# Attention, dense layer and routed experts on one core: the hand-over from the dense layer's last chunk to expert 0 is rearranged

## The chip, the cores and the metric

The kernel runs on 1 core of one Trainium2 chip. The metric is device time in microseconds of one execution. Three runs of the kernel before took 890.3, 893.34 and 895.14 us.

## What is computed

Three layers follow one another. The first is attention with local windows and 32 global tokens. Its output, as 2176 rows of 512 numbers, goes through a dense layer with a hidden size of 2048; its activation is a leaky ReLU with a slope for each hidden unit. The third layer sends each row to one of 8 experts, 272 rows (`CAP`) to each, by a greedy choice over all gate values:

```python
# attention: out_g for 32 global tokens, out_l with |i - j| <= 32 and the global tokens
x = attention(q_l, k_l, v_l, q_g, k_g, v_g)          # -> [2176, 512]
h = x @ w_in                                         # 512 -> 2048
x = (maximum(h, 0) + alpha * minimum(h, 0)) @ w_out  # 2048 -> 512
logits = x @ w_gate                                  # 8 experts
for idx in argsort(-logits.flatten()):               # greedy, cap = 272
    tok, e = idx // 8, idx % 8
    if assigned[tok] < 0 and counts[e] < cap: assign tok to e
for e in range(8):
    out[rows of e] = maximum(x[rows of e] @ w1[e], 0) @ w2[e]   # 512 -> 1024 -> 512
```

## The kernel before

All matrix products of the dense layer and of the experts are made of three: a number is split into a rounded part and a rest (`split`, L67: a cast on ScalarE, ACT, and a subtraction on VectorE, DVE, or on GpSimd, POOL), and high times high, high times low and low times high are summed in one PSUM bank. The 2176 rows are worked on as 8 chunks of 272 (`CH`). Features lie on the partitions, rows on the free axis.

**Order of the work.** The dense layer's hidden units are taken in two halves. The first half runs beside attention. Of the second half all first products and the gate's logits are computed before any second product, so that the routing can begin early. The second products of that half are `gemm2b` (L1066): for each chunk c, four blocks of 128 output features, two at a time (d2 = 0, then 2), with the two accumulations j = 0, 1 interleaved over the hidden blocks f. At the end of each pair DVE adds the sums to the part that the first half left (`xo`). While a chunk runs, a list `post` of small jobs is worked off, one for every second f: the rows of the chunk before.

**Rows.** `rows(c, xo, q)` (L214) turns a chunk from features to rows, in blocks of 128, 128 and 16 rows (`blk`): four PE transposes into a PSUM bank (`yt`), a copy on ACT into `yr`, a DMA on the queue of SyncE (SP) to `x2d` in DRAM. The 16 left-over rows of every chunk are collected in one tile `xtail` of 128 rows, and written once, after the last chunk, by one strided DMA (L227). The bank is `px`, tag `tx`, of which there is one; only the left-over block takes another (`pH`, two banks; `p4` has two as well).

**Routing.** `router` is a generator that issues a step of a search each time that `advance(dt)` has counted enough estimated time: a group of nine small matmuls (`pc`, L795) or one (`pa`, L807) and DVE work behind each. It writes an expert's number (`EID`, L845) and its rows (`IDS`, L751).

**Experts.** `fetch_1` and `fetch_2` (L911, L922) load an expert's `w1` and `w2` in four parts each into a buffer `raw3` (pool `rw`, two buffers), and split them: cast on ACT, subtraction on POOL into the tile `m`, of 2.4 us. `fetch_x` (L903) gathers the expert's rows out of `x2d` with three indirect DMAs that POOL issues, `gather` (L932) turns each block by four transposes into a bank (`xt`, again `px`, tag `tx`) and splits it into `xsh`, `xsl`. `up` and `down` are the expert's two products, each accumulation in one of the four banks of `pH` and `p4`. Expert k+1's weights are loaded while expert k runs, as soon as the routing has named it and the weight tile is free.

**Between the two.** After the last chunk the remaining `post` jobs are worked off. `fetch_2(0)` and `fetch_x(0)` follow, then `NB0` = 20 pairs of matmuls on constants (`busy`, 512 columns each, into a bank that nobody reads) with router steps between them, then `gather(0)` with four more such matmuls behind each block. `fetch_1(1)` is then held behind the last row copy on ACT and the last gather on POOL:

```python
        for x in gather(0):
            busy(idle, ones, 4)
            advance(x + 0.9)
        with tc.issue_after(last_rows[0].ins), tc.issue_after(st.ins):
            while closed[0] < 2:
                force()
            fetch_1(1)
```

The order on PE is the order in the program (`manual_schedule`, L1054). The order on the other engines and in the DMA queues is worked out by a planner from estimated costs: an instruction whose inputs are ready can be put ahead of others that stand earlier in the program. Once planned, each engine executes in order.

Of the kernel before, what the change touches and what calls it, by code (L numbers as in the profile page):

```python
# [9 lines left out]
F32 = mybir.dt.float32  # L10
# [5 lines left out]
OP = mybir.AluOpType  # L16
# [9 lines left out]
def tile_attention_moe_moe(ctx: ExitStack, tc: tile.TileContext, qkw, vw,  # L26
                           w_in, w_out, alpha, w_gate, w1, w2, out):
    nc = tc.nc
    V, A, P, T = nc.vector, nc.scalar, nc.gpsimd, nc.tensor
    B, H, S, D, SG = BHSDG  # L30
    DM, DF = w_in.shape
    E, _, FF = w1.shape
    NTOK = B * (S + SG)
# [3 lines left out]
    KD = DM // 128  # L37
# [5 lines left out]
    KH = KF // 2  # L43
    CH = CAP
# [22 lines left out]
    def split(hi, lo, src, lo_eng=None):  # L67
        a = A.copy(hi, src)  # L68
        return a, (lo_eng or V).tensor_tensor(lo, src, hi.bitcast(F32), op=OP.subtract)  # L69
# [137 lines left out]
            yield 0.7  # L207
        X[c, hf] = None

    last_rows = [None]  # L210
    tail = {}
    blk = [(0, 128), (128, 256), (256, CH)]

    def rows(c, xo, q):  # L214
        a, b = blk[q]
        end = c == NCH - 1
        if q == 2 and not end:
            A.copy(tail["x"][:, :, 16 * c:16 * c + 16], xo[:, :, a:b])
            return
        pool, tag = (pH, "h1") if end and q == 2 else (px, "tx")  # L220
        t = pool.tile([128, DM], F32, name="yt", tag=tag)
        for k in range(KD):
            T.transpose(t[:, k * 128:(k + 1) * 128], tail["x"][:, k] if q == 2 else xo[:, k, a:b], ident)  # L223
        r = gx2.tile([128, DM], F32, name="yr", bufs=3)
        last_rows[0] = A.copy(r, t)
        if q == 2:
            nc.sync.dma_start(out=x2d.rearrange("(c r) d -> c r d", r=CH)[:, a:b], in_=r)  # L227
        else:
            nc.sync.dma_start(out=x2d[c * CH + a:c * CH + b], in_=r)

    LR = 512
    LT = KD + KH

# [342 lines left out]
    with ExitStack() as mo:  # L576
# [120 lines left out]
        gm.close()  # L697

        rt = mo.enter_context(tc.tile_pool(name="rt", bufs=2))
        rw = mo.enter_context(tc.tile_pool(name="rw3", bufs=2))  # L700
        EID = rc_.tile([128, E], I32, name="EID")
        IDS = rc_.tile([128, E, 3], I32, name="IDS")
        TT = rc_.tile([128, 2, E], F32, name="TT")
# [218 lines left out]
        def fetch_2(k):  # L922
            pool, nm = ((wa, "wa0") if k % 2 == 0 else (wb, "wb1"))
            t2 = pool.tile([128, 2, K3, DM], F32R, name="m2", tag=nm)
            w2e = w2[bass.ds(SLOT[k]["er"], 1)].rearrange("e (k p) f -> p (e k) f", p=128)
            for kk in range(0, K3, 2):
                raw = rw.tile([128, 2, DM], F32, name="raw3")
                nc.sync.dma_start(out=raw, in_=w2e[:, kk:kk + 2])
                split(t2[:, 0, kk:kk + 2], t2[:, 1, kk:kk + 2], raw, lo_eng=P)
            SLOT[k]["w2"] = t2  # L930

        def gather(k):  # L932
            d = SLOT[k]
            xh = sl.tile([128, KD, CAP], F32R, name="xsh")
            xl = sl.tile([128, KD, CAP], F32R, name="xsl")
            d["x"] = (xh, xl)
            for q, (a, b) in enumerate(SEG):
                n = b - a
                t = px.tile([128, KD, 128], F32, name="xt", tag="tx")
                for kk in range(KD):  # L940
                    T.transpose(t[:, kk, :n], d["xg"][:n, q, kk * 128:(kk + 1) * 128], ident[:n, :n])  # L941
                split(xh[:, :, a:b], xl[:, :, a:b], t[:, :, :n])
                yield 0.45 if q < 2 else 0.1

        def up(k, f):
# [91 lines left out]
        def advance(dt):  # L1037
            if wait[0] is None:
                return False
            wait[0] -= dt  # L1040
            while wait[0] is not None and wait[0] <= 0:
                x = next(route, None)
                wait[0] = None if x is None else max(wait[0], -0.3) + x * SLK
            return True
# [3 lines left out]
            advance(0)  # L1048

        HB = {}  # L1050
        NB0 = 20
        SLK, SLK2 = 1.0, 1.0
        GA = 17.5
        mo.enter_context(tc.manual_schedule(engines={mybir.EngineType.PE}))  # L1054
# [11 lines left out]
        def gemm2b(c):  # L1066
            xo = X[c, 1]
            nxt = [lambda f=f: splitg(c + 1, f) for f in range(KH)] if c + 1 < NCH else []
            if nxt:
                loadp(c + 1)  # L1070
            wo = WO[1]
            for d2 in range(0, KD, 2):
                ps = [(p4 if d2 else pH).tile([128, CH], F32, name="h2", tag="h4" if d2 else "h1") for _ in range(2)]
                for f in range(KH):
                    hi, lo = HB[c][f]
                    for j in range(2):
                        ds_ = slice((d2 + j) * 128, (d2 + j + 1) * 128)
                        for a, (w, x) in enumerate(((0, hi), (0, lo), (1, hi))):
                            T.matmul(ps[j], wo[:, w, f, ds_], x, start=f == 0 and a == 0, stop=f == KH - 1 and a == 2)  # L1079
                            if a < 2 or j == 0:  # L1080
                                yield 0.113
                    if (f % 2 == 1 if c != DEF[0] else d2 or f) and post:
                        post.pop(0)()
                        yield 0.4
                    if nxt and ((d2 == 0 and f % 2) or (d2 and f >= 2)):
                        nxt.pop(0)()
                    yield 0.113
                if "x" not in tail:
                    tail["x"] = gb_.tile([128, KD, 128], F32, name="xtail")
                for j in range(2):  # L1090
                    m = 256 if c == NCH - 1 else CH
                    V.tensor_tensor(xo[:, d2 + j, :m], ps[j][:, :m], xo[:, d2 + j, :m], op=OP.add)
                    if m < CH:
                        V.tensor_tensor(tail["x"][:, d2 + j, 16 * c:], ps[j][:, m:], xo[:, d2 + j, m:], op=OP.add)
            for q in range(3):
                post.append(lambda q=q: rows(c, xo, q))

        with tc.tile_pool(name="gb_", bufs=1) as gb_:
            NR = 14
            gr = wb.tile([128, 2, NR, CH], F32R, name="gr", tag="wb0")  # L1100
            loadp(DEF[0])
            for f in range(KH):
                splitg(DEF[0], f)
            post.pop(0)()
            for j, c in enumerate(DEF):
                for x in gemm2b(c):
                    if j or not post:
                        advance(x)
                    if closed[0] >= 1 and j >= 4 and 0 not in SLOT:
                        fetch_1(0)  # L1110
            for f in post:
                f()
                advance(0.5)
            while closed[0] < 1:
                force()
            if 0 not in SLOT:
                fetch_1(0)
        g2.close()
        sl = mo.enter_context(tc.tile_pool(name="sl", bufs=1))
        fetch_2(0)  # L1120
        while listed[0] < 1:
            force()
        st = fetch_x(0)
# [4 lines left out]
        for x in gather(0):  # L1128
            busy(idle, ones, 4)
            advance(x + 0.9)  # L1130
        with tc.issue_after(last_rows[0].ins), tc.issue_after(st.ins):
            while closed[0] < 2:
                force()
            fetch_1(1)
# [103 lines left out]
```

## Time and profile before

| | us |
|---|---|
| median of three runs | 893.34 |
| the profiled execution | 892.66 |
| its span | 890.9 |
| PE busy with matmuls | 840.3 (94%) |
| DVE busy | 531.7 (60%) |
| ACT busy | 371.6 (42%) |
| POOL busy | 350.5 (39%) |

Times in a view are microseconds from the start of the span. The profiled execution's own time is 1.8 us above its span. PE is the engine of the matmuls, PEld the loading of their weights, which goes on beside them; the ends of matmuls are modelled. PEclk is the clock granted to TensorE: 1.00 is 2.4 GHz, 0.50 is 1.2 GHz. The page shows the span in 40 slices of 22.3 us, a digit for each tenth of busy time:

```profile
PE   6989899999999899999999999999798989899995
POOL 2234320111104543400000728370767777877811
```

An arrow `<-` in brackets behind an instruction names what ended the idle time before it. "xN" is a count of like instructions merged into one row; the duration then is the whole group's.

### The profile page before, as it was taken

What the parts mean: (1) busy time and instruction counts of PE and PEld (TensorE: products, weight loads), DVE (VectorE), ACT (ScalarE), POOL (GpSimd) and SP (SyncE); (2) the same over time, 40 slices, a digit from 0 to 9 for tenths busy, and PEclk for the clock granted to TensorE, in tenths of its full rate; (3) what the DMA queues carried; (4) which work ended last, traced back from release to release, by engine and by line L of the source; (5) the groups of instructions that cost most, each with busy time, mean ns of one, the idle gap of its engine ahead of it and who ended that gap; (6) DMA issues with size and microseconds to landing.
All of it is one profiled execution on the core that took longest, in us unless ns stands there. A gap on an engine that the chain in (4) does not pass through costs nothing. (4 is left out here: it accounts for less than half of the span.)

```text
span 890.9 us, 18514 instructions
## 1 busy us (share of the span) xinstructions
PE 840.3 (94%) x7168; PEld 761.3 (85%) x7168; DVE 531.7 (60%) x1776; ACT 371.6 (42%) x872; POOL 350.5 (39%) x299
## 2 busy tenths in 40 slices
PE   6989899999999899999999999999798989899995
PEld 4768798888898899998989898997598989899995
DVE  5999955556639776565655566766566676511120
ACT  5977656455534443210100334242244444445431
POOL 2234320111104543400000728370767777877811
PEclk8999999999999999999999999999999999999999
DMA  8574514413034342201321235332455455555500
GB/s 284 192 271 155 148 43 154 120 51 117 33 116 157 108 127 94 70 8 54 98 56 45 78 112 178 91 104 81 125 147 185 144 166 179 157 165 179 180 24 36
DMA packets 50272, 107.64 MB, mean 121 GB/s; under 512 B 6729, under 2 KB 23113, under 8 KB 50185
## 3 DMA queue, kind: packets, MB, share of 16 engines
q1 hardware_dynamic: 47288, 97.56, 35.3%
q0 software_dynamic: 2896, 8.92, 2.7%
q8 instruction: 56, 0.92, 0.4%
q14 instruction: 32, 0.25, 0.1%
HBM read 88.63 MB, written 17.83 MB: 119 GB/s over the span
## 5 line engine op out<-in xcount | busy, mean ns | idle before, releaser
L69 POOL TENSOR_TENSOR m<-raw,m 128x1024 fp32r<-128x1024 f32 x64 | 152.6, 2391 | 58.8 <-ACT m L68 55.9
L168 PE MATMUL h<-xh,win 128*128 128x272 f32 x768 | 165.6, 298 | 2.2 <-DVE g L187 1.9
L168 PEld LDWEIGHTS h<-xh,win 128*128 128x128 f32 x768 | 126.4, 190 | 11.3 <-issue 6.3
L69 POOL TENSOR_TENSOR glo<-g,ghi 128x272 fp32r<-128x272 f32 x64 | 57.1, 896 | 169.2 <-ACT ghi L68 169.2
L200 PE MATMUL y<-ghi,wout 128*128 128x272 f32 x512 | 110.9, 297 | 2.7 <-ACT wout L68 1.3
L168 PE MATMUL h<-xl,win 128*128 128x272 f32 x384 | 111.8, 292 | 1.7 <-DVE xl L69 1.5
L1079 PE MATMUL h<-gr,wout 128*128 128x272 f32 x768 | 110.7, 295 | 0.0
L955 PE MATMUL h<-xsh,m 128*128 128x272 f32 x512 | 106.6, 298 | 1.9 <-ACT xsh L68 1.9
L173 DVE TENSOR_SCALAR nm<-h,al 128x272 f32<-128x272 f32 x128 | 63.5, 497 | 74.3 <-PE h L168 73.8
L69 POOL TENSOR_TENSOR gr<-gb,gr 128x272 fp32r<-128x272 f32 x64 | 48.0, 777 | 145.2 <-DVE nm L173 114.9
L68 ACT CAST m<-raw 128x1024 fp32r<-128x1024 f32 x64 | 66.9, 1049 | 88.9 <-DMA raw<-in_moe_w_dram 87.4
L971 PE MATMUL h<-hh,m 128*128 128x272 f32 x512 | 103.4, 293 | 0.0
L1079 PEld LDWEIGHTS h<-gr,wout 128*128 128x128 f32 x768 | 99.2, 188 | 0.9 <-ACT gr L68 0.4
L200 PEld LDWEIGHTS y<-ghi,wout 128*128 128x128 f32 x512 | 83.5, 189 | 8.4 <-issue 3.6
L955 PEld LDWEIGHTS h<-xsh,m 128*128 128x128 f32 x512 | 83.3, 191 | 3.2 <-ACT xsh L68 2.0
L971 PEld LDWEIGHTS h<-hh,m 128*128 128x128 f32 x512 | 81.4, 188 | 0.5 <-issue 0.2
L200 PE MATMUL y<-glo,wout 128*128 128x272 f32 x256 | 74.8, 297 | 1.4 <-POOL glo L69 1.4
L971 PE MATMUL h<-hl,m 128*128 128x272 f32 x256 | 75.5, 295 | 0.0
L168 PEld LDWEIGHTS h<-xl,win 128*128 128x128 f32 x384 | 72.9, 190 | 3.0 <-DVE xl L69 2.6
L955 PE MATMUL h<-xsl,m 128*128 128x272 f32 x256 | 75.3, 294 | 0.2 <-DVE xsl L69 0.2
L344 ACT ACTIVATE pr<-sc,mx 128x224 f32<-128x224 f32 x128 | 60.5, 475 | 26.1 <-DVE mx L342 25.9
L342 DVE CUSTOM_DVE_ANT_0 sc<-s,mask 128x224 f32<-128x224 f32 x128 | 43.5, 383 | 28.7 <-PE s L336 28.7
(226 smaller groups left out, 1567.2 us busy)
## 6 DMA issues: line engine op xcount, KB each, us to landing
raw<-in_moe_w_dram SPq DMA_DIRECT2D x64, 512.0 KB, 3.8
qk<-in_qk_dram SPq DMA_DIRECT2D x15, 736.0 KB, 5.0
vv<-in_v_dram SPq DMA_DIRECT2D x16, 512.0 KB, 5.0
raw<-in_moe_w_in_dram SPq DMA_DIRECT2D x16, 512.0 KB, 5.4
raw<-in_moe_w_out_dram SPq DMA_DIRECT2D x16, 512.0 KB, 3.8
xs<-xb SPq DMA_DIRECT2D x16, 272.0 KB, 4.5
xpart<-xd SPq DMA_DIRECT2D x32, 136.0 KB, 1.8
xb<-xs SPq DMA_DIRECT2D x8, 544.0 KB, 3.9
```

The lines of the kernel that those rows point to most:

```text
L68: a = A.copy(hi, src)
L69: return a, (lo_eng or V).tensor_tensor(lo, src, hi.bitcast(F32), op=OP.subtract)
L168: T.matmul(ps, wi[:, w, k, fs], x[:, k], start=i == 0, stop=i == 3 * KD - 1)
L173: epi[0] = V.tensor_scalar(nm, ps, 0.0, al[:, hf * KH + f:hf * KH + f + 1], op0=OP.min, op1=OP.mult)
L200: T.matmul(ps, wo[:, w, f, ds_], x[:, f], start=i == 0, stop=i == 3 * KH - 1)
L342: V.tensor_tensor_reduce(out=sc, in0=s[h][:, ii], in1=m, scale=-D ** -0.5, scalar=BIG, op0=OP.add, op1=OP.min, accum_out=d["mx"][:, h, i:i ...
L344: A.activation(out=d["pr"][:, h, i], in_=sc, func=AF.Exp, bias=d["mx"][:, h, i:i + 1], scale=-1.0, accum_out=d["sm"][:, h, i:i + 1])
L955: T.matmul(ps, d["w1"][:, w, kk, fs], x[:, kk], start=i == 0, stop=i == 3 * KD - 1)
L971: T.matmul(ps, d["w2"][:, w, f, ms], x[:, f], start=i == 0, stop=i == 3 * K3 - 1)
L1079: T.matmul(ps[j], wo[:, w, f, ds_], x, start=f == 0 and a == 0, stop=f == KH - 1 and a == 2)
```

## The change

- `rows` writes only whole blocks of 128 rows, and copies a chunk's left-over rows into `xtail`, which now has 112 rows (seven chunks). A new job `tails` transposes and writes those 112 rows as the fourth `post` job of the last chunk. The last chunk's own 16 rows are written by themselves.
- In the last chunk, the second pair of output blocks isn't interleaved any more: first j = 0 over all f, its add on DVE, then j = 1. During j = 1 no router step is issued (it yields `None`), and at f = 4 the transposes of the output blocks 0 to 2 are issued for all three row blocks (`last_blocks`), into three banks (`px` and two of `pH`). The last block's transposes follow its add. `last_out` copies the three banks, the middle one on DVE, the others on ACT, and issues three writes.
- The gathered rows of expert 0 go through three banks (`px`, `p4`, `pH`).
- The raw buffers are three instead of two. `fetch_2(0)` stands at the start of the last chunk in the program, if expert 0's `w1` has been fetched.
- `NB0` is 12, and `fetch_1(1)` is held behind the last cast of `gather(0)` instead of behind the last row copy.

```diff
@@ rows, tails, last_blocks, last_out
-        pool, tag = (pH, "h1") if end and q == 2 else (px, "tx")
-        t = pool.tile([128, DM], F32, name="yt", tag=tag)
+        t = px.tile([128, DM], F32, name="yt", tag="tx")
...
+    def tails():
+        n = 16 * (NCH - 1)
+        t = px.tile([128, DM], F32, name="yt", tag="tx")
+        for k in range(KD):
+            T.transpose(t[:n, k * 128:(k + 1) * 128], tail["x"][:, k], ident)
+        r = gx2.tile([128, DM], F32, name="yr", bufs=3)
+        A.copy(r[:n], t[:n])
+        nc.sync.dma_start(out=x2d.rearrange("(c r) d -> c r d", r=CH)[:NCH - 1, 256:], in_=r[:n])
+
+    def last_blocks(xo, ks):
+        for q, (a, b) in enumerate(blk):
+            if q not in yts:
+                pool, tag = (pH, "h1") if q else (px, "tx")
+                yts[q] = pool.tile([128, DM], F32, name="yt", tag=tag)
+            for k in ks:
+                T.transpose(yts[q][:b - a, k * 128:(k + 1) * 128], xo[:, k, a:b], ident)
+
+    def last_out():
+        for q, (a, b) in enumerate(blk):
+            r = gx2.tile([128, DM], F32, name="yr", bufs=3)
+            (V.tensor_copy if q == 1 else A.copy)(r[:b - a], yts[q][:b - a])
+            nc.sync.dma_start(out=x2d[NTOK - CH + a:NTOK - CH + b], in_=r[:b - a])
@@ raw buffers
-        rw = mo.enter_context(tc.tile_pool(name="rw3", bufs=2))
+        rw = mo.enter_context(tc.tile_pool(name="rw3", bufs=3))
@@ gather
-                t = px.tile([128, KD, 128], F32, name="xt", tag="tx")
+                pool, tag = ((px, "tx"), (p4, "h4"), (pH, "h1"))[q] if k == 0 else (px, "tx")
+                t = pool.tile([128, KD, 128], F32, name="xt", tag=tag)
...
-                split(xh[:, :, a:b], xl[:, :, a:b], t[:, :, :n])
+                d["cast"] = split(xh[:, :, a:b], xl[:, :, a:b], t[:, :, :n])[0]
@@ gemm2b
-        NB0 = 20
+        NB0 = 12
...
+                if end and d2:
+                    for j in range(2):
+                        for f in range(KH):
+                            for x in step(f, j):
+                                yield None if j else x
+                            if j and f == 4:
+                                last_blocks(xo, range(KD - 1))
+                        add(j)
+                    last_blocks(xo, [KD - 1])
+                    last_out()
+                    return
...
+            if c == NCH - 2:
+                post.append(tails)
@@ after the chunks
                 for x in gemm2b(c):
-                    if j or not post:
+                    if x is not None and (j or not post):
                         advance(x)
                     if closed[0] >= 1 and j >= 4 and 0 not in SLOT:
                         fetch_1(0)
-            for f in post:
-                f()
-                advance(0.5)
+                    if j == NDEF - 1 and 0 in SLOT and "w2" not in SLOT[0]:
+                        fetch_2(0)
...
-        with tc.issue_after(last_rows[0].ins), tc.issue_after(st.ins):
+        with tc.issue_after(SLOT[0]["cast"].ins), tc.issue_after(st.ins):
```

In `gemm2b`, `step` holds the three matmuls of one f and j, and `add` the addition to `xo`, which before was cut at row 256 in the last chunk.

## Rows read from the trace of the kernel before

**Rows 1.** Busy time by stretch: us, each engine's busy time, PEclk, DMA share, GB/s

```profile
639.30:881.40 242.10, 231.62 (x1931) 222.04 (x1929) 109.31 (x429) 105.50 (x189) 159.69 (x88) 0.99 0.47 145
...
639.30:641.30 2.00, 2.00 (x12) 1.68 (x11) 1.23 (x5) 0.00 (x0) 1.43 (x2) 0.60 0.72 171
...
671.70:674.80 3.10, 3.10 (x21) 2.99 (x21) 0.47 (x3) 1.11 (x2) 2.77 (x3) 0.50 0.79 272
```

**Rows 2.** The chain of waits, 615 to 640: start, us, what

```profile
616.65 0.43 DVE pt L1092
...
619.67 0.60 ACT yr L225
...
620.29 4.23 DMA x2d<-yr
...
625.50 0.75 POOL xg L906
...
631.49 3.66 DMA raw<-in_moe_w_dram
```

**Rows 3.** The timeline of PE, last chunk and rows: start, us, instruction, idle before

```profile
615.31 0.38 PE L795 MATMUL pc<-ohs,gs 128*128 128x16 bf16 x9
...
615.55 0.37 PE L1079 MATMUL h<-gr,wout 128*128 128x272 f32 x1
...
618.45 0.66 PE L223 MATMUL yt<-ident,pt 128*128 128x128 f32 x4 [1.00 <-ACT yr L225]
...
618.95 0.60 PE L223 MATMUL yt<-ident,xtail 128*128 128x128 f32 x4
```

**Rows 4.** The timeline of all engines at the kernel's end

```profile
881.83 0.44 PE L989 MATMUL ox<-ident,ot 128*128 128x128 f32 x2 [0.46 <-ACT ot L978]
...
882.19 1.07 ACT L1003 COPY orow<-ox 128x512 f32<-128x512 f32 x2 [0.42 <-PE ox L989]
...
882.30 0.69 DVE L1003 COPY orow<-ox 128x512 f32<-128x512 f32 x1 [0.32 <-PE ox L989]
```

**Rows 5.** DMA issues, 617 to 620.1, 624 to 626.4, 628 to 629: KB, us to landing

```profile
x2d<-yr SPq DMA_DIRECT2D x2, 256.0 KB, 2.0
...
xg<-x2d,IDS POOLq DMA_INDIRECT x1, 3.6
...
xg<-x2d,IDS POOLq DMA_INDIRECT x1, 2.8
```

**Rows 6.** The timeline of all engines, the hand-over

```profile
619.59 1.90 PE L88 MATMUL idle<-ones 128*128 128x512 bf16 x8
...
628.21 0.87 POOL L906 DMA_INDIRECT xg<-x2d,IDS  x1 [0.30 <-issue]
...
629.00 1.02 PE L88 MATMUL idle<-ones 128*128 128x512 bf16 x4
...
631.96 0.66 PE L941 MATMUL xt<-ident,xg 128*128 128x128 f32 x4 [0.53 <-DVE xsl L69]
...
635.18 1.04 ACT L68 CAST m<-raw 128x1024 fp32r<-128x1024 f32 x1 [4.06 <-DMA raw<-in_moe_w_dram]
...
637.49 0.60 PE L941 MATMUL xt<-ident,xg 16*128 16x16 f32 x4 [4.01 <-DVE xsl L69]
...
639.35 0.79 PE L955 MATMUL h<-xsh,m 128*128 128x272 f32 x1
```

**Rows 7.** The timeline of POOL, weights: the subtractions of a split

```profile
597.90 2.40 POOL L69 TENSOR_TENSOR m<-raw,m 128x1024 fp32r<-128x1024 f32 x1 [1.19 <-ACT m L68]
...
642.20 4.78 POOL L69 TENSOR_TENSOR m<-raw,m 128x1024 fp32r<-128x1024 f32 x2
```

**Rows 8.** Waits of ACT, 639 to 860: us in total, times, longest

```profile
ACT m L68 <- DMA raw<-in_moe_w_dram: 71.2, 48, 3.3
```

**Rows 9.** The timeline of PE and ACT ahead of up(1)

```profile
670.16 1.04 ACT L68 CAST m<-raw 128x1024 fp32r<-128x1024 f32 x1 [2.46 <-DMA raw<-in_moe_w_dram]
...
671.66 0.59 PE L955 MATMUL h<-xsh,m 128*128 128x272 f32 x1 [1.87 <-ACT xsh L68]
```

More of the change, by code (lines that the diff above doesn't have):

```diff
@@ L208, in gemm @@
         X[c, hf] = None
-    last_rows = [None]
     tail = {}
@@ L215, in rows @@
         a, b = blk[q]
-        end = c == NCH - 1
-        if q == 2 and not end:
+        if q == 2:
             A.copy(tail["x"][:, :, 16 * c:16 * c + 16], xo[:, :, a:b])
             return
-        pool, tag = (pH, "h1") if end and q == 2 else (px, "tx")
-        t = pool.tile([128, DM], F32, name="yt", tag=tag)
+        t = px.tile([128, DM], F32, name="yt", tag="tx")
         for k in range(KD):
-            T.transpose(t[:, k * 128:(k + 1) * 128], tail["x"][:, k] if q == 2 else xo[:, k, a:b], ident)
+            T.transpose(t[:, k * 128:(k + 1) * 128], xo[:, k, a:b], ident)
         r = gx2.tile([128, DM], F32, name="yr", bufs=3)
[L225 to L229, printed above, removed]
+        A.copy(r, t)
+        nc.sync.dma_start(out=x2d[c * CH + a:c * CH + b], in_=r)
+    def tails():
[18 more added lines that the diff above has]
+            nc.sync.dma_start(out=x2d[NTOK - CH + a:NTOK - CH + b], in_=r[:b - a])
+    yts = {}
     LR = 512
@@ L1071, in gemm2b, with step, add @@
             wo = WO[1]
+            end = c == NCH - 1
+            if "x" not in tail:
+                tail["x"] = gb_.tile([128, KD, 16 * (NCH - 1)], F32, name="xtail")
             for d2 in range(0, KD, 2):
                 ps = [(p4 if d2 else pH).tile([128, CH], F32, name="h2", tag="h4" if d2 else "h1") for _ in range(2)]
+                def step(f, j):
+                    hi, lo = HB[c][f]
+                    ds_ = slice((d2 + j) * 128, (d2 + j + 1) * 128)
+                    for a, (w, x) in enumerate(((0, hi), (0, lo), (1, hi))):
+                        T.matmul(ps[j], wo[:, w, f, ds_], x, start=f == 0 and a == 0, stop=f == KH - 1 and a == 2)
+                        if a < 2 or not j:
+                            yield 0.113
+                def add(j):
+                    V.tensor_tensor(xo[:, d2 + j], ps[j], xo[:, d2 + j], op=OP.add)
+                if end and d2:
[9 more added lines that the diff above has]
+                    return
                 for f in range(KH):
-                    hi, lo = HB[c][f]
                     for j in range(2):
[L1077 to L1081, printed above, removed]
+                        yield from step(f, j)
                     if (f % 2 == 1 if c != DEF[0] else d2 or f) and post:
@@ L1087, in gemm2b @@
                     yield 0.113
-                if "x" not in tail:
-                    tail["x"] = gb_.tile([128, KD, 128], F32, name="xtail")
                 for j in range(2):
[L1091 to L1094, printed above, removed]
+                    add(j)
             for q in range(3):
                 post.append(lambda q=q: rows(c, xo, q))
+            if c == NCH - 2:
+                post.append(tails)
         with tc.tile_pool(name="gb_", bufs=1) as gb_:
@@ L1119, in tile_attention_moe_moe @@
         sl = mo.enter_context(tc.tile_pool(name="sl", bufs=1))
-        fetch_2(0)
+        if "w2" not in SLOT[0]:
+            fetch_2(0)
         while listed[0] < 1:
```

## The prediction, made before the result was known

> **What bounds the kernel now.** I read four views. The page gives a span of 890.9 us; the profiled execution took 892.66 us, 1.8 more, and the three runs have a median of 893.34, so I work in the profiled execution and add 0.7 at the end. Its 40 slices show a TensorE that is busy at 8 or 9 tenths nearly everywhere in the second half, but for one slice of 7, which begins at 624 us. The stretch view then cuts the end of the kernel in two: a hand-over, from the last matmul of the last `gemm2b` chunk (615.92) to the first matmul of expert 0 (639.35), 23.4 us in which no wanted matmul runs except transposes and a little routing, and the expert stage, 639.3 to 881.4, where PE is busy 231.6 of 242.1 us [rows 1]. So PE sets the end: what the hand-over loses, the end gets, and in the expert stage 10.5 us of idle time and some clock can be won, no more.
>
> The chain of waits says what the hand-over consists of [rows 2]: the last add ends at 617.08, row copies follow one another until 620.27, the write of the left-over rows lands at 624.52, and the gather on POOL starts at 625.50. Behind that the timeline shows [rows 6]: transposes of the second gathered block at 631.96, of the third only at 637.49, after 4.01 us of waiting; the first up-matmul at 639.35.
>
> **The change, part by part, as a sum of times.**
>
> *End of the matmuls.* Four transposes of the early tail write and nine of `last_blocks` now stand inside the last chunk. Two groups of four start 0.50 apart [rows 3], so one is 0.125 and thirteen are 1.6. The last tile issues no router step; the stretch it replaces held one `pc` group, 0.24 to the next matmul [rows 3], and one `pa`, about half of that: 0.35 on PE. 615.92 becomes 617.2. The transposes at f = 4 of j = 1 wait for the add of j = 0; fifteen matmuls, 1.8 us at 0.12 each [rows 1], cover its 0.43, and if a router operation held it on DVE past them, all of PE would stand behind it; I count nothing.
>
> *Last add to last row copy.* Before: 615.92 to 620.27, 4.35 us: two adds with router work between them, then three blocks through a single `tx` bank, the second waiting 1.00 for the copy of the first [rows 2, 3]. After: one add is left, 0.43 [rows 2], and then three transposes into three banks with copies on two engines. The end of the kernel has that layout already: transposes at 881.83, two ACT copies in 1.07 until 883.26, the DVE copy 0.69 beside them [rows 4], 1.43 in all. With the hops 2.0, so 619.2. Bounds: 1.9 with no hop; 2.7 if the add again begins 0.73 after the last matmul's end, as the second add did (616.65 against 615.92) [rows 2, 3].
>
> *Row writes.* The last write before is strided over eight chunks and takes 4.23 from its issue [rows 2]; the two plain block writes ahead of it landed in 2.0 [rows 5]. After, the last is 16 adjacent rows; its nearest row is the plain block, and I take 2.0, with 4.23 as the other end. The strided write goes out half a chunk earlier, with 48 matmuls still to come, some 5.8 us, and costs nothing; were it late, it would be the same 4.23. SP issues three writes instead of two and one, each beside a copy; no weight load can stand ahead of them there, since the next free raw buffer needs POOL, which waits for these writes. Landing 621.2. POOL took 0.98 from landing to first gather [rows 2]: 622.2 against 625.50.
>
> *Gather.* Block 0 lands 3.6 after its issue, the third is issued 2.71 after the first and lands 2.8 later [rows 2, 5, 6]: 625.8 and 627.7; the second in between. PE: forty fillers with router steps ran from 619.59 to 630.02 [rows 6], so twenty-four take 6.3; from about 618.1 they end at 624.4, and PE waits 1.4 for block 0. Transposes 0.5 and four fillers 1.0 per block, three times: 625.8 + 4.5 = 630.3, plus one router step: 630.6. That needs two waits gone. One is the bank: block 1 waited for the DVE part of block 0 [rows 6], now it has its own. The other is the long one: ACT executes in order, and its cast of block 1 stood behind a weight cast of expert 1 that waited 4.06 for a DMA [rows 6], which itself could only be issued when POOL had freed one of two raw buffers at 631.49 [rows 2]. After, all of expert 1's first casts are ordered behind the last cast of the gather. What is late next is the gather's landing, not ACT: a block's cast and subtraction, about what the copies of as many columns at the end take, 0.54 and 0.69 [rows 4], fit in the 1.5 us per block. First up-matmul 630.6 against 639.35: **-8.7**. With both bounds on the bad side (2.7 and 4.23) it is -5.8; with the filler the limit and no wait, -9.7.
>
> *Clock.* Before, the up-matmuls began at a granted clock of 0.60 over 2.0 us, a loss of 0.8, after 4.01 us without a matmul [rows 1, 6]. After 1.87 us of idle time near 670 the clock was at 0.50 for 3.1 us, a loss of 1.55 [rows 1, 9]. The 1.4 us that PE will wait for block 0 is near the second case; then transposes and fillers run at half speed. I take half of 1.55 as lost and 0.8 as won: **0**, between -0.8 and +0.8. The Trainium skill, in "TensorE: Matmul & The Clock Gate", Part 1, holds that the throttled clock is the default and only activity releases it, which speaks against sixteen fillers fewer; by it the whole 1.55 is lost and the sum is 0.8 higher. The two rows show that idle time is followed by the lower of the two levels, not that this idle time will be.
>
> *Router.* Eight filler pairs of 0.43 and three calls of 0.5 are gone from the hand-over, 4.9 us of router time, about 1.6 steps of some 0.35 on PE, now in the expert stage: **+0.6**. The lists are far enough ahead: nothing waits for them.
>
> *Weights.* That expert 0's `w2` is split in the last chunk is worth nothing: the trace has its last split at 597.90, before that chunk begins [rows 7]; the planner had pulled it forward already. Expert 1's `w1` does lose its cover, the hand-over. Its last part ran at 642.20 and up(1) starts at 671.66 [rows 7, 9]. Now four subtracts of 2.4 start at about 631, with three gathers between, and end near 643; up(1) comes near 663. The slack falls from 27 to 20 us and nothing is late.
>
> *Third raw buffer.* All through the expert stage ACT waits for raw weights, 48 times, 71.2 us, 1.48 each [rows 8], because a load starts only when the subtract two parts back has ended. With three buffers it starts one subtract, 2.4 us, earlier, more than the mean wait. PE feels only some of it: before up(1) ACT stood 2.46 us at such a cast with the cast of the gathered block behind it, PE idled 1.87 and lost 1.55 by the clock [rows 1, 9]. Of 10.5 idle and 1.6 of clock I take a third: **-4**. Bounds: -8 if all such stalls go, +4 if casts are only placed earlier in ACT's order and stand there as long.
>
> *Sum:* -8.7 + 0 + 0.6 - 4 = -12.1, 880.6 in the profiled execution, **881** as a median.
>
> **Rivals.**
> A. *Given back in expert 0 and 1.* The gap is won, but four casts of expert 1 now meet the `hh` activations on ACT, and the fourth waits a DMA of 3.66 [rows 2]. If ACT stands longer than the four result banks cover, PE stalls once, at the price of the stall before up(1), 3.4, and the third buffer gives nothing: 892.66 - 8.7 + 0.6 + 3.4 = 888. For it: the casts move out of an idle stretch. Against: 231.62 us for 1931 PE instructions is 0.12 each [rows 1], twelve to a bank, so four banks are some 5.8 us.
> B. *The third buffer clears the stage.* -8.7 + 0.6 - 8 - 0.8: 876. For it: the wait of 1.48 is less than the 2.4 that the load gains. Against: some PE waits are for the router's DVE chain.
> C. *Slower.* Weight casts placed by the planner for three buffers stand ahead of `hh` and `xsh` on ACT, each waiting for its load. At one stall of 3.4 for each of experts 1 to 7 that is 23.8 against 8.1 won: 908. It decides from the third stall on. Against: no load can begin later than it does now.
> D. *The hand-over isn't shortened:* the gather would still start near 625 and ACT's order would still hold a block back. Then -1 to +1: 893. For it: POOL's wait covers all writes to `x2d`, so one late write keeps it; against: the early write has 48 matmuls and the last rows to land behind.
>
> **How the numbers follow.** Forecast 0.62, A 0.14, B 0.14, C 0.05, D 0.05. About 0.5% (4.5 us) is what a measurement here can tell from no change, so faster means below 888.9. The forecast and B are faster; A lies at the edge and I give it two thirds: 0.86 faster. The rest of A and D are the same: 0.09; slower 0.05. The range takes the forecast's bounds (gap -5.8 to -9.7, stage -8 to +1) and stops short of C and D: 874 to 889.
>
> **What would show it.** Right: first gather near 622, three gathered blocks transposed about 1.5 us apart, first up-matmul at 629 to 632, ACT's waits for raw weights under 50 us in the expert stage, PE idle there under 8. Wrong: the 16-row write landing after 4 us, the clock at 0.5 well into up(0), the cast of a gathered block standing behind a weight cast, or a PE wait for ACT in up(0) or before up(1).

## The result, and the profile after

The changed kernel takes 878.87 us (877.69 to 880.3, 4 runs) against 894.24 (890.3 to 895.21, 4 runs) for the kernel before on the same chip: a ratio of 0.9837 [0.9802, 0.9872]. The forecast was 881, with a range of 874 to 889. The profiled execution took 877.69 with a span of 875.7, 15.2 less than before.

In the tables "hand-over" runs from the end of the last `gemm2b` matmul to the first up-matmul of expert 0, "stage" from there to the end of the last down-matmul.

| profiled execution, us | before | after | difference |
|---|---|---|---|
| up to the last chunk, the same work in both | 601.10 | 600.08 | -1.0 |
| last chunk | 14.80 | 15.52 | +0.7 |
| hand-over | 23.43 | 13.63 | -9.8 |
| stage | 242.02 | 236.91 | -5.1 |
| behind it | 9.5 | 9.5 | 0 |

The first line is no gain of the change: like instructions already stand 1.0 earlier before anything differs. So 14.2 are to be explained. The page of the changed kernel, busy time and then the slices that answer to those of before; the slice of 7 is gone:

```profile
PE 835.0 (95%) x7156; PEld 760.4 (87%) x7156; DVE 531.8 (61%) x1773; ACT 370.1 (42%) x872; POOL 350.3 (40%) x299
...
PE   6989999999999999999999999999899999999995
```

The view by stretch, in the columns of [rows 1]: the last chunk; the hand-over; in it the wait for the first gathered block and the transposes behind that; the first 2 us of expert 0; the whole stage:

```profile
600.08:615.60 15.52, 15.52 (x138) 14.88 (x137) 9.60 (x39) 2.01 (x4) 0.00 (x0) 1.00 0.16 50
...
615.60:629.24 13.64, 10.93 (x83) 5.82 (x82) 8.28 (x30) 2.81 (x6) 3.32 (x4) 1.00 0.27 83
...
622.50:624.70 2.20, 0.04 (x1) 0.02 (x1) 0.54 (x3) 0.00 (x0) 1.77 (x2) 1.00 0.62 153
624.70:627.00 2.30, 2.29 (x23) 1.69 (x24) 0.85 (x2) 0.65 (x2) 0.00 (x0) 1.00 0.32 103
...
629.24:631.24 2.00, 2.00 (x23) 1.92 (x22) 1.09 (x5) 2.00 (x3) 1.55 (x2) 1.00 0.30 51
...
629.24:866.15 236.91, 230.19 (x1952) 221.13 (x1950) 114.89 (x459) 107.40 (x193) 166.19 (x91) 1.00 0.49 151
```

The granted clock is 1.00 all through the hand-over and into expert 0, where it was 0.60 [rows 1]. In the stage PE idles 6.7 (236.91 less 230.19) instead of 10.5.

The timeline of all engines, from the last add to the first gather. Three transposes wait 0.53 for the add; two copies go on ACT and one beside them on DVE; the last ends at 617.61, 2.0 behind the last matmul (615.61). Before, copies followed one another until 4.35 behind it. Behind the first gather the profile names a router step on DVE as what ended its wait; but the gather starts 5.4 to 5.6 behind the last matmul in every kernel with the new rows, whatever is named there, and in e6 it is the write of the rows:

```profile
615.66 0.44 DVE L1106 TENSOR_TENSOR pt<-h,pt 128x272 f32<-128x272 f32 x1 [3.54 <-PE h L1101]
616.15 0.55 PE L240 MATMUL yt<-ident,pt 128*128 128x128 f32 x3 [0.53 <-DVE pt L1106]
616.56 1.05 ACT L245 COPY yr<-yt 128x512 f32<-128x512 f32 x2 [7.62 <-PE yt L240]
616.68 0.69 DVE L245 COPY yr<-yt 128x512 f32<-128x512 f32 x1 [0.58 <-PE yt L240]
617.17 1.31 SPq L246 DMA_DIRECT2D x2d<-yr  x3
...
620.99 1.15 POOL L924 DMA_INDIRECT xg<-x2d,IDS  x1 [23.70 <-DVE sat L818]
```

The DMA issues between 616.9 and 618.6 (KB, us to landing) show the 16-row write to take what the whole blocks took [rows 5], instead of the 4.23 of the strided one [rows 2]:

```profile
x2d<-yr SPq DMA_DIRECT2D x2, 256.0 KB, 2.3
x2d<-yr SPq DMA_DIRECT2D x1, 32.0 KB, 2.0
```

The timeline of PE and then of ACT, to be held against [rows 6]. Three gathered blocks are transposed at 624.71, 626.26 and 628.20, the first after 2.17 us for which the profile names no releaser; the block's gather was issued 3.7 earlier, and one took 3.6 to land [rows 5]. On ACT the three casts of a gathered block come first, and expert 1's weight casts stand behind the last of them:

```profile
621.07 1.47 PE L88 MATMUL idle<-ones 128*128 128x512 bf16 x6
...
624.71 0.63 PE L960 MATMUL xt<-ident,xg 128*128 128x128 f32 x4 [2.17 <-issue]
...
626.26 0.64 PE L960 MATMUL xt<-ident,xg 128*128 128x128 f32 x4
...
628.20 0.42 PE L960 MATMUL xt<-ident,xg 16*128 16x16 f32 x4
...
629.24 0.47 PE L974 MATMUL h<-xsh,m 128*128 128x272 f32 x1
```

```profile
625.49 0.58 ACT L68 CAST xsh<-xt 128x512 fp32r<-128x512 f32 x1 [7.88 <-PE xt L960]
626.94 0.58 ACT L68 CAST xsh<-xt 128x512 fp32r<-128x512 f32 x1 [0.86 <-PE xt L960]
628.65 0.21 ACT L68 CAST xsh<-xt 128x64 fp32r<-128x64 f32 x1 [1.13 <-PE xt L960]
628.76 2.94 ACT L68 CAST m<-raw 128x1024 fp32r<-128x1024 f32 x3
```

The waits in the stage (us in total, times, longest), of ACT for raw weights, which were 71.2 and 48 [rows 8], and of PE before up(1), which was 1.87 [rows 9]:

```profile
ACT m L68 <- DMA raw<-in_moe_w_dram: 21.6, 19, 2.3
```

```profile
PE h L974 <- ACT xsh L68: 1.3, 1, 1.3
```

This wait too has a weight cast ahead of it on ACT, which waited 1.35 for its load:

```profile
659.87 1.04 ACT L68 CAST m<-raw 128x1024 fp32r<-128x1024 f32 x1 [1.35 <-DMA raw<-in_moe_w_dram]
...
661.10 0.21 ACT L68 CAST xsh<-xt 128x64 fp32r<-128x64 f32 x1
```

### The profile page after: what moved, and what is told of

Read it like the earlier page. It is cut to its first block, busy times and chain, and to the rows that moved or that the text cites. A ratio compares the mean times of both kernels' runs of the same rounds, so it can differ in the third digit from the quotient of the medians.

```text
span 875.7 us, 18487 instructions
## 1 busy us (share of the span) xinstructions
PE 835.0 (95%) x7156; PEld 760.4 (87%) x7156; DVE 531.8 (61%) x1773; ACT 370.1 (42%) x872; POOL 350.3 (40%) x299
## 5 line engine op out<-in xcount | busy, mean ns | idle before, releaser
L974 PEld LDWEIGHTS h<-xsh,m 128*128 128x128 f32 x512 | 82.3, 188 | 2.7 <-ACT xsh L68 1.4
```

What stands on the lines that cost most here:

```text
L974: T.matmul(ps, d["w1"][:, w, kk, fs], x[:, kk], start=i == 0, stop=i == 3 * KD - 1)
```

## The experiments

A total moves by 3 to 8 us between executions of one program, so the lengths of hand-over and stage are set beside the totals. They come from one profiled execution of each kernel, whose own time is given too, since it can lie some us off the median (e6's lies 5.9 below it, e11's 4.6 above). Each ratio is against the kernel before on the same chip.

| kernel | median us | ratio | profiled, us | hand-over | stage | raw buffers |
|---|---|---|---|---|---|---|
| before | 894.24 | | 892.66 | 23.43 | 242.02 | 2 |
| after | 878.87 | 0.9837 [0.9802, 0.9872] | 877.69 | 13.63 | 236.91 | 3 |
| e1_two_raw | 889.01 | 0.9951 [0.9925, 0.9977] | 891.47 | 14.02 | 247.90 | 2 |
| e2_three_raw_only | 888.68 | 0.9937 [0.9912, 0.9962] | 891.14 | 23.77 | 239.46 | 3 |
| e11_hold_only | 891.24 | 0.9973 [0.995, 0.9996] | 895.88 | 20.74 | 246.52 | 2 |
| e8_rows_alone | 891.41 | 0.9976 [0.9953, 0.9999] | 891.01 | 19.95 | 244.06 | 2 |
| e4_old_hold | 878.24 | 0.9823 [0.9797, 0.9849] | 878.55 | 13.63 | 237.76 | 3 |
| e3_one_bank | 880.23 | 0.9845 [0.9814, 0.9876] | 879.95 | 14.28 | 238.81 | 3 |
| e10_one_bank_old_hold | 880.5 | 0.986 [0.982, 0.99] | 880.28 | 14.24 | 239.88 | 3 |
| e5_filler20 | 879.39 | 0.9862 [0.9833, 0.9891] | 876.85 | 15.84 | 237.29 | 3 |
| e6_filler4 | 882.14 | 0.9891 [0.9867, 0.9914] | 876.27 | 14.63 | 238.31 | 3 |
| e7_no_early_w2 | 876.61 | 0.9828 [0.9804, 0.9852] | 876.02 | 13.54 | 238.09 | 3 |
| e12_half_parts | 880.18 | 0.9866 [0.9824, 0.9908] | 876.78 | 15.39 | 237.60 | 6 halves |
| e13_lean | 875.49 | 0.98 [0.9763, 0.9837] | 878.21 | 12.96 | 238.77 | 3 |

### The third raw buffer, out of the change and by itself

e1 takes it out of the changed kernel, e2 puts it alone into the kernel before:

```diff
-        rw = mo.enter_context(tc.tile_pool(name="rw3", bufs=3))
+        rw = mo.enter_context(tc.tile_pool(name="rw3", bufs=2))
```

> The changed kernel with two raw buffers, all else kept. Hand-over means last dense matmul to first matmul of expert 0 (23.4 us before, 13.6 after); stage means first to last matmul of the experts (242.0 before, 236.9 after). Theory 1, the third buffer is what shortens the stage, by taking ACT's waits for raw weights away: the stage is 241 to 243 again, ACT waits 60 to 75 us for raw weights, the hand-over stays near 13.6, the total is 883 to 885. Rival, the stage is shorter because it begins earlier and at full clock: stage 237 to 238.5, total 879 to 880.

Measured: 889.01. The hand-over hardly moves (14.02), the stage grows to 247.90, 11 above the changed kernel and 5.9 above the kernel before. Theory 1 had the direction, but not the size. By stretch, the whole stage of this kernel and then three parts of it:

```profile
632.29:880.19 247.90, 236.75 (x1952) 226.83 (x1950) 115.28 (x459) 107.99 (x193) 167.10 (x91) 0.97 0.48 146
...
664.29:672.29 8.00, 7.49 (x49) 7.17 (x50) 1.97 (x11) 2.65 (x7) 7.46 (x5) 0.58 0.68 186
728.29:736.29 8.00, 6.83 (x47) 6.28 (x47) 3.88 (x15) 3.72 (x7) 6.81 (x6) 0.79 0.53 193
776.29:784.29 8.00, 5.53 (x37) 4.96 (x36) 3.04 (x11) 3.06 (x6) 5.79 (x4) 0.79 0.53 174
```

The same 1952 PE instructions are busy 6.6 longer than in the changed kernel (236.75 against 230.19), at a clock of 0.97; the other 4.4 are idle time. The timeline shows what stands ahead of the first and the last of the three parts: up(1) waits 2.13 for a cast that stood behind a weight cast waiting 2.66 for its load, and a routing step waits 2.47 for DVE:

```profile
663.30 1.04 ACT L68 CAST m<-raw 128x1024 fp32r<-128x1024 f32 x1 [2.66 <-DMA raw<-in_moe_w_dram]
664.80 0.59 PE L974 MATMUL h<-xsh,m 128*128 128x272 f32 x1 [2.13 <-ACT xsh L68]
...
779.48 0.47 PE L758 MATMUL pl<-vas,sbs 128*48 128x68 bf16 x9 [2.47 <-DVE sbs L753]
```

So in this profile more time goes to the slower clock than to idle time, and not every wait ahead of it is for a load. How typical that is, isn't shown: this execution lies 2.5 above the median, and its mean granted clock is 0.975 where the kernel's other four executions had 0.982 to 0.989. ACT waits for raw weights 66.4 us in the stage, against 21.6.

> The kernel before with three raw buffers and nothing else. Theory 1, the third buffer works in the stage alone, and the cast that holds the gathered block back in the hand-over (4.06 us) still stands there, since the fourth part still needs POOL: hand-over near 23.4, stage 237 to 238, total 888 to 890. Rival, the third buffer by itself frees the hand-over too, because the load that the cast waits for is out before the gather: hand-over 19 to 20, total 884 to 886.

Measured: 888.68, the stage 2.6 shorter, the hand-over as before. The long wait stays: a weight cast still waits for its load ahead of the third gathered block's transposes (638.32). Two rows of ACT, then ACT's waits in the stage:

```profile
636.01 1.04 ACT L68 CAST m<-raw 128x1024 fp32r<-128x1024 f32 x1 [3.45 <-DMA raw<-in_moe_w_dram]
636.96 0.58 ACT L68 CAST xsh<-xt 128x512 fp32r<-128x512 f32 x1
```

```profile
ACT m L68 <- DMA raw<-in_moe_w_dram: 17.6, 16, 2.0
```

Theory 1 holds for the hand-over, which the third buffer doesn't shorten; the stage missed its 237 to 238. Three quarters of ACT's waits are gone, yet in this profile PE gains only 2.6. One reason is that up(1) waits 3.08 here, longer than before: three weight casts in a row, none of them waiting for a load, stand on ACT ahead of the cast that it needs:

```profile
670.58 2.94 ACT L68 CAST m<-raw 128x1024 fp32r<-128x1024 f32 x3
673.41 0.21 ACT L68 CAST xsh<-xt 128x64 fp32r<-128x64 f32 x1
```

By the stages of the profiles the same buffer is worth 2.6 in the kernel before and 11 in the changed one. By the totals it is 5.6 (3.4 to 7.9) and about 10 (6 to 14, from the ratios of e1 and of the changed kernel with their intervals). So it is worth more in the changed kernel, but the contrast is smaller than the two pairs of profiles make it, and by the totals alone it is at the edge of the noise.

### Parts of the hand-over with two raw buffers

e11 puts the new hold alone into the kernel before; e8 keeps of the change only the rows (one bank, two buffers, `NB0` 20, the hold behind the last row copy, `w2` where it was):

```diff
-        with tc.issue_after(last_rows[0].ins), tc.issue_after(st.ins):
+        with tc.issue_after(SLOT[0]["cast"].ins), tc.issue_after(st.ins):
```

> The kernel before with the new hold alone: expert 1's first casts behind the last cast of the gather; two raw buffers, one bank, old rows, 20 filler pairs. Theory 1, the long wait goes from the hand-over (23.4 to 19 or 20), but the casts and subtractions that ran there now stand in the expert stage with only two raw buffers, which gives it back as in the changed kernel with two raw buffers (stage 245 to 248): total 892 to 895, no gain. Rival, the stage keeps its 242: total 889 to 890.

Measured: 891.24. The hand-over is 2.7 shorter, since no weight cast stands between the gathered blocks any more (on ACT two of them run at 637.47, behind the last). The stage is 4.5 longer:

```profile
637.94:884.46 246.52, 234.00 (x1931) 224.30 (x1929) 110.23 (x429) 109.46 (x193) 166.88 (x91) 0.98 0.47 147
```

In this profile what was won is given back, as Theory 1 had it. The total doesn't bear that out: hand-over and stage of the profile together lose 1.8, but this execution lies 4.6 above the median, and by its ratio the kernel is 2.4 faster than the kernel before (0.4 to 4.5), which is nearly the whole gain of the hand-over. Theory 1 expected 892 or more; neither theory is settled.

> The row part alone: left-over rows in two writes, last tiles one by one, row blocks in three banks; one bank for the gathered blocks, two raw buffers, 20 filler pairs, the old hold and the old place of w2's load. Theory 1, the row part moves the gather on POOL by 3 to 4 us and no more, and the long wait stays behind it: hand-over 19.5 to 21, stage 242, total 889.5 to 891.5. Rival, what the rows win is lost at once, since the held-back block waits for the same raw load: hand-over 23, total 893 to 894.

Measured: 891.41, the hand-over 3.5 shorter, as Theory 1 said, the stage 2.0 longer, which it did not say. The first gather starts at 621.21, but the third block's transposes wait until 633.17: the cast of block 1 again stands behind a weight cast on ACT:

```profile
630.86 1.04 ACT L68 CAST m<-raw 128x1024 fp32r<-128x1024 f32 x1 [2.56 <-DMA raw<-in_moe_w_dram]
631.81 0.58 ACT L68 CAST xsh<-xt 128x512 fp32r<-128x512 f32 x1
```

Over all kernels the stage takes 242.0 to 247.9 with two buffers (4 profiles) and 236.9 to 239.9 with three, or six halves (10). Where the hand-over is as before, the two differ by 2.6; where it is shorter, by 8 (246.2, the mean of e1, e8 and e11, against 238.2, the mean of the changed kernel and the seven drawn from it with three whole buffers).

### What removed the long wait on ACT

e4 holds `fetch_1(1)` behind the last row copy again, e3 lets the gathered rows go through one bank again, e10 does both:

```diff
+            yts["last"] = (V.tensor_copy if q == 1 else A.copy)(r[:b - a], yts[q][:b - a])
...
-        with tc.issue_after(SLOT[0]["cast"].ins), tc.issue_after(st.ins):
+        with tc.issue_after(yts["last"].ins), tc.issue_after(st.ins):
```

```diff
-                pool, tag = ((px, "tx"), (p4, "h4"), (pH, "h1"))[q] if k == 0 else (px, "tx")
+                pool, tag = px, "tx"
```

> The changed kernel with expert 1's first casts held behind the last row copy on ACT, as before, instead of behind the last cast of the gather. Theory 1, ACT's order made the long wait and the new hold removed it: three casts run in the idle hand-over, but the fourth stands on ACT for a load that POOL frees only behind the gather, so a gathered block waits again: hand-over 16.5 to 18.5, total 882 to 884. Rival, with three raw buffers the hold is of no use: hand-over 13.6, stage up to 1 us shorter, total 878 to 879.

Measured: 878.24, the hand-over 13.63, to the hundredth that of the changed kernel. The theory fell and its rival stands, but for the stage, which is 0.9 longer and not shorter. ACT in this kernel: three weight casts run as soon as the row copies are done, and the fourth, which waits for a load, was put behind the last cast of the gather:

```profile
617.49 2.93 ACT L68 CAST m<-raw 128x1024 fp32r<-128x1024 f32 x3
...
628.64 0.21 ACT L68 CAST xsh<-xt 128x64 fp32r<-128x64 f32 x1 [1.13 <-PE xt L960]
...
630.68 1.05 ACT L68 CAST m<-raw 128x1024 fp32r<-128x1024 f32 x1 [1.83 <-DMA raw<-in_moe_w_dram]
```

> The changed kernel with the gathered blocks of expert 0 through one bank again. Theory 1, the bank costs only the wait of a block's transposes for the subtraction of the block before (626.84 instead of 626.26, and so on): hand-over 14.3 to 14.9, total 879.5 to 880.5. Rival, the banks are what took the long wait out of the hand-over: hand-over 17 or more, total 882 or more.

Measured: 880.23, the hand-over 0.65 longer, since block 1 waits 0.45 for the DVE part of block 0. That is Theory 1; the total can't show it.

> The changed kernel with one bank for the gathered blocks and with the old hold, three raw buffers kept. Each alone left the hand-over at 14.3 and 13.6 us. Theory 1, bank and hold stand in for each other: with one bank the planner expects the second block late and puts the fourth weight cast ahead of its cast on ACT, as in the kernel before; only the new hold or the three banks keep it behind. Hand-over 17 to 19, total 882 to 884. Rival, the long wait is gone for another reason (the earlier gather): hand-over 14.3 to 15, total 879 to 881.

Measured: 880.5, the hand-over 14.24, no more than with one bank alone. Theory 1, that bank and hold stand in for each other, fell. The fourth cast again stands behind the gather's last (628.22):

```profile
629.47 1.05 ACT L68 CAST m<-raw 128x1024 fp32r<-128x1024 f32 x1 [1.04 <-DMA raw<-in_moe_w_dram]
```

Neither the third buffer alone (e2) nor the rows alone (e8) removes the long wait; with both, the shorter filler and the early `w2` it is gone without hold and banks (e10). Which of the remaining parts the planner needed for that order wasn't run.

### The filler

```diff
-        NB0 = 12
+        NB0 = 20    # e5; e6: NB0 = 4
```

> The changed kernel with 20 filler pairs instead of 12. Theory 1, the filler's length now sets when the gathered rows are turned: 40 fillers and the router steps between them take 10.4 us, so the first transposes come near 627 instead of 624.7, hand-over 15.6 to 16.1, total 880.5 to 882. Rival, the landing of the gather sets it whatever the filler does: hand-over 13.6, total 879.

Measured: 879.39, the hand-over 2.2 longer: the first gathered block is transposed at 623.40, 5.9 behind its gather, against 3.7 in the changed kernel. There the filler is the limit. The hand-over is as Theory 1 said; the total is within the noise of the changed kernel's.

> The changed kernel with 4 filler pairs instead of 12. PE then has no work for some 6 us before the gathered rows land. Theory 1, the idle time lowers the granted clock to 0.5 and it stays there into up(0), as in the kernel before after 4.01 us: hand-over 14.5 to 15.5 and about 0.8 more in the stage, total 880 to 881.5. Rival, the four matmuls behind each block bring the clock back in time: total 878.5 to 879.5.

Measured: 882.14, the hand-over 1.0 longer. PE idles 6.16 (timeline), and the stretches show the transposes at half speed, most of the clock back in the next 2.6 us, and up(0) at full speed:

```profile
621.08 1.08 PE L960 MATMUL xt<-ident,xg 128*128 128x128 f32 x4 [6.16 <-DMA xg<-x2d,IDS]
```

```profile
621.00:623.90 2.90, 2.82 (x15) 1.68 (x16) 0.69 (x1) 0.59 (x1) 0.00 (x0) 0.50 0.21 76
623.90:626.50 2.60, 2.60 (x24) 1.55 (x21) 1.44 (x8) 1.14 (x3) 0.32 (x1) 0.95 0.02 6
626.50:628.50 2.00, 2.00 (x23) 1.91 (x22) 1.53 (x7) 2.00 (x3) 1.59 (x2) 1.00 0.24 45
```

In this execution that part of Theory 1 by which the slow clock lasts into up(0) was wrong, and the gap costs about 1 us in the hand-over. The kernel's other four executions took at least 5.6 us longer than this one; what the gap cost in them isn't shown.

### Expert 0's `w2`, smaller raw parts, and a leaner hand-over

e7 takes out the two lines that call `fetch_2(0)` in the last chunk.

> The changed kernel without the new place of the load of expert 0's w2. Theory 1, worth nothing, since the planner had pulled the load forward already: last subtraction of w2 near 593 to 598 as in both kernels, total 878 to 880. Rival, without it the planner leaves the splits for the hand-over once there are three raw buffers: the subtractions run behind the gather on POOL and down(0) is late: total 882 or more.

Measured: 876.61, a little less than expected, hand-over 13.54, stage 238.09. The last subtraction of expert 0's `w2` ends at 593.12, 19.7 ahead of the last matmul of the last chunk; in the changed kernel it ends 19.8 ahead. The early place is worth nothing.

e12 cuts each raw part in two (six buffers of 512 columns, the same memory, loads and splits half as large; the same for `w2`):

```diff
-                raw = rw.tile([128, FF], F32, name="raw3")
-                nc.sync.dma_start(out=raw, in_=w1e[:, kk])
-                split(t1[:, 0, kk], t1[:, 1, kk], raw, lo_eng=P)
+                for h in range(2):
+                    hs = slice(h * FF // 2, (h + 1) * FF // 2)
+                    raw = rw.tile([128, FF // 2], F32, name="raw3")
+                    nc.sync.dma_start(out=raw, in_=w1e[:, kk, hs])
+                    split(t1[:, 0, kk, hs], t1[:, 1, kk, hs], raw, lo_eng=P)
```

> The changed kernel with each weight part halved: six raw buffers of 512 columns instead of three of 1024, twice as many loads, casts and subtractions. Theory 1, what ACT and POOL still wait for is the latency of a load, and the finer grain hides more of it in the same space: ACT's waits for raw weights (21.6 us) under 15, PE idle in the stage 5 to 6 instead of 6.7, total 876 to 878.5. Rival, the fixed cost of twice as many instructions on ACT and POOL and more places where a cast stands in front of an activation: total 880 to 885.

Measured: 880.18, the stage 237.60, ACT's raw waits 22.0 in 26 pieces instead of 21.6 in 19, PE idle 7.4 instead of 6.7. The theory fell: the finer grain brings no gain in the stage, and the hand-over is 1.8 longer.

e13 goes without the new hold and the early `w2`, and thins out what stands behind each gathered block:

```diff
-            busy(idle, ones, 4)
-            advance(x + 0.9)
+            busy(idle, ones, 2)
+            advance(x + 0.5)
```

> The changed kernel with the old hold, without the new place of w2's load, and with two instead of four filler matmuls (and 0.4 us less router time) behind each gathered block. Theory 1, between the blocks the fillers and router steps and not the landing set the pace (third block turned at 628.2 though it landed near 626.5): hand-over 12.3 to 13, stage as with the old hold, 237 to 238, total 877 to 878.5. Rival, the shorter filler leaves PE idle and the clock falls: hand-over 13.6 or more and 1 us more in the stage, total 879 to 881.

Measured: 875.49, the lowest median, hand-over 12.96 as Theory 1 had it, blocks at 624.10, 625.59 and 626.61. Its stage, 238.77, is above what Theory 1 said and 1.9 longer than the changed kernel's, and its interval [0.9763, 0.9837] overlaps that kernel's, so that it beats the changed kernel isn't shown.

## Why the prediction was right, and which of its terms were not

*Last add to last row copy, row writes, gather: right.* Shifted by the 1.0 that the profile lies earlier, the first gather starts at 622.0 (622.2 said) and the first up-matmul at 630.26 (630.6). The copies take 2.0 as said and the 16-row write 2.0, so the bound of 4.23 fell away. PE waits 2.17 for block 0 where 1.4 was said, and the last chunk costs 0.7 and not 1.28; that nearly cancels. The bank was rightly named but is worth only 0.65 (e3). One bound was added up wrongly: without the wait of 1.4 the hand-over term comes to -10.1 and not to -9.7.

*The long wait: right that it goes, wrong why.* The prediction gave it to the new order behind the last cast of the gather. The hold does this in the kernel before (e11), but in the changed kernel the wait stays away without it (e4), even with the single bank (e10). An order on ACT is a planner's result, and the parts of the change overlap in producing it.

*Clock: mis-sized, 0 said.* The 0.8 of the first up-matmuls was won and nothing lost: PE idled 2.17 and the granted clock stayed at 1.00 in every stretch shown above. The Trainium skill, in "TensorE: Matmul & The Clock Gate", Part 1, holds that the throttled state is the default and that activity releases it; it doesn't say that a wait as short as this one throttles, which the prediction read into it. By that reading, with 0.8 more lost, the sum would have been too high by a further 0.8. The trace of the changed kernel shows no throttling there, while e6, after 6.16 us of idle time, shows 0.50, as the page would have it.

*Router +0.6:* not measured by itself. 21 PE instructions more lie in the stage (1952 against 1931), yet PE is busy there 1.4 less, since the slow stretches are gone.

*Weights: right for expert 1's `w1`, but what comes behind it was put at nothing.* The last subtraction of that `w1` ends at 641.95 and up(1) starts at 661.37, so the slack is 19.4 where 20 was said, and it isn't late. It was no measure of the weights that follow: with two buffers and a shorter hand-over the stage is longer by 2.0 (e8), 4.5 (e11) and 5.9 (e1) in the profiles. The totals make this clear for e1 alone, where of the 9.4 won in the hand-over, less some 0.7 for the last chunk, 4.4 (2.1 to 6.7) are left. That is rival A's direction and about its price, but not its place. I cut the stage of three kernels at the starts of up(1), up(2) and up(5): before 32.3, 33.0, 94.4 and 82.3; e1 32.5, 33.2, 99.5 and 82.7; the changed kernel 32.1, 30.8, 92.7 and 81.3. Against the kernel before e1 loses 5.0 of its 5.9 in experts 2 to 4, and 0.2 in each of experts 0 and 1, where A had it. Of the 5.0, 3.4 lie in up(4), which holds the router's wait of 2.47 and the slow clock behind it (19.56 against 16.18).

*Third raw buffer: direction right, size wrong in its setting.* Said was -4. By itself it is -2.6 in the stage of the profile and -5.6 in the total (e2); in the changed kernel it is -11 and about -10, because it also saves what two buffers would have given back. The stage as a whole, -5.1, is near the -3.4 that the terms gave (0.6 and -4), because the two errors nearly cancel; so far the number came out by luck. Without the buffer -8.7 of the hand-over would have bought some 4 us in total (e1: 0.9951 of 894.24 is 889.9).

*Rivals.* A fell only through the buffer. B wanted a stage cleared of waits: 6.7 us of idle time stay, and up(1) still waits 1.3. A PE wait for ACT before up(1) was also named as a sign of being wrong; it came, but shorter than the 1.87 of before, and the granted clock stayed at 1.00 behind it. For C, the casts didn't pile up: 19 waits instead of 48; its mechanism shows once in e2, in the three casts ahead of up(1). D fell with the first gather.

Open is what the slower stage with two buffers consists of, row by row. Two of the waits behind which e1's clock fell are for ACT (2.13, and 1.17 at 731.63), one of 2.47 is the router's; whether the router's came from the loads or by chance, one profile doesn't show.

## What to carry to other kernels

A gap that is closed was also a place where later loads and splits ran unseen: before it is shortened, look at what runs in it for the next stage, and give that work its own room first, here a third staging buffer, by the totals worth 5.6 alone and about 10 beside the shorter gap. Two changes that are worth 4 and 6 apart were worth 15 together, if only just beyond the noise, so take each out of the whole as well as putting it alone into the kernel before. A stage read from one profile is to be held against the times of the other executions, since it can be an untypical one. A wait named at an engine in order is to be read as a place in its queue: ask which instruction stands ahead, and what that one waits for.

## What the runs showed of the hardware that was not expected

- Waits of like length had unlike prices: after 2.17 us of idle time in the hand-over the granted clock stayed at 1.00; in e1 a wait of 2.13 stood ahead of 8 us at 0.58, and in the kernel before one of 1.87 ahead of 3.1 us at 0.50 [rows 1, 9]. After 6.16 us (e6) it was 0.50 for 2.9 us.
- A write of 16 rows and 32 KB lands no sooner than one of 128 rows and 256 KB: 2.0 against 2.0 to 2.3 [rows 5]. The strided write of as many bytes as a block took 4.23 [rows 2], and 4.15 and 4.18 in e2 and e11. While it was under way the 16 DMA engines were busy 0.45 of the time, against 0.77 behind the last plain writes of the changed kernel (618.10 to 620.10). That the stride is the cause isn't shown: single blocks took 2.0 to 4.4 over the whole kernel before.
